# Sketched attention with a gated feed-forward on one core: weights loaded as fp32 and cast on chip, the first denominators made another way, and every engine's order written anew

## The chip, the cores and the metric

The kernel runs on one core of a Trainium2 chip. The metric is device microseconds of one launch; smaller is better. A core has TensorE (matrix products, in the profile PE, its weight loads PEld), VectorE (DVE), ScalarE (ACT), GpSimd (POOL) and SyncE (SP), which here only issues transfers. Products land in eight PSUM banks of 128 x 512 fp32. VectorE and ScalarE read them; GpSimd works here on SBUF alone.

## What is computed

Cut to what matters, the reference is:

```python
def phi(x):                       # S1, S2: 8 x 32
    a = einsum('rd,bhsd->bhsr', S1, x)
    b = einsum('rd,bhsd->bhsr', S2, x)
    return outer(a, b)            # 64 features for each row
q_p, k_p = phi(q), phi(k)         # q, k, v: 4 batches, 4 heads, 1088 rows, 32
kv  = einsum('bhsf,bhsd->bhfd', k_p, v)
z   = sum(k_p, axis=rows)
num = einsum('bhsf,bhfd->bhsd', q_p, kv)
den = einsum('bhsf,bhf->bhs', q_p, z) + 1e-6
x   = (num / den) as [4352, 128]
out = (relu(x @ w_gate) * (x @ w_val)) @ w_out      # 128 -> 1536 -> 128
```

## The kernel before

**Attention.** Rows of a batch lie in 34 columns of 32 rows on 128 partitions (four heads by 32). A batch's keys are transposed (`kt1`, lines 484 to 491), sketched with S1 and S2 (`ksk`, line 501), transposed back (`kt2`, line 507) and multiplied out to 64 features (`kphi`, line 543). `z` (line 515) sums the features, `w` and `wc` (528, 532) fold it back into a third sketch of 8 numbers, and `kv` (567) and `kve` (573) make the 64 x 32 table of each head. The queries follow (class Q): transposed (`qt1`, 987), sketched with three sketches at once (`qsk`, 780), transposed back (`qt2`, 793), and the denominator is a product and a sum of two of the sketches (`bw` 801, `red` 807, `rd` 811); `an` (815) divides, `qphi` (821) multiplies out, a transpose and `num` (848) give x, and ScalarE copies it to `xT` (861). The first half of batch 0 goes another way (class First, line 589), so that x is there sooner: its denominators come from `aT`, `csk` and a reciprocal that is spread over 32 columns and transposed (`rx`, `rT`), and `xd` (715) multiplies numerator and reciprocal.

**Feed-forward.** 4352 rows are cut into groups of 256 or 512 columns of `xT`. A unit (class F) is 512 columns of work: a gate product g and a value product v (line 916, each 512 columns in one or two matmuls), `relu` on ScalarE (921), the product of both, h, and four output matmuls o (944). h is one VectorE operation that reads v from PSUM (931), or, for the units in `POOL_UNITS`, a ScalarE copy of v (`vcp`, 925) and a GpSimd product (`hp`, 936). There are 102 units. Three blocks of each weight (g, v, o; t = 0 to 2) serve 512 hidden columns each. When a group has had its twelve hidden blocks, ScalarE scales the result (`oe`, 951) and four transfers store it.

**Weights.** Block 0 of each weight is loaded as fp32 by SyncE into tiles that are still free (`q_abc`) and cast by ScalarE (line 316). The other six are loaded by GpSimd's queue, which casts on the way (line 310). Their place is set by `RINGS`: behind the GpSimd product `kphi 0 8`, and a one-element GpSimd write called gate (line 391) keeps the load of batch 1's keys back until the fourth of them is issued.

**Order.** All operations are listed in one plan. `START` gives each a number; sorted by it they are emitted, and each engine takes its own in that order, strictly one after the other. `BANKS` gives each product its PSUM bank. `WARM` puts in matmuls of zeros (line 1015), 55 in all, 29 of them ahead of the first sketch.

Of the kernel before, what the change touches and what calls it, by code (L numbers as in the profile page):

```python
# [23 lines left out]
POOL_UNITS = [7, 8, 9, 10, 14, 15, 17, 23, 31, 43, 44, 47, 54, 64, 71, 74, 81, 94, 96]  # L24
KBC = [(2, 4), (4, 8)]
WL = {'g0': 'SP', 'v0': 'SP', 'o0': 'SP', 'g1': 'POOL', 'v1': 'POOL', 'o1': 'POOL', 'g2': 'POOL', 'v2': 'POOL', 'o2': 'POOL'}
V0L = [['SP', 'SP', 'SP', 'SP'], ['SP', 'SP', 'SP', 'SP']]
FILL = 'DVE'
RINGS = [['ld s1', 'ld s2', 'ld k01', 'ld v000', 'ld v001', 'ld v002', 'ld v003', 'ld v010', 'ld v011', 'ld v012', 'ld v013'], ['mz', 'kt1 0 0'], ['fills', 'kt1 0 0'], ['zero', 'fills'], ['ld k00', 'ld q00', 'table'], ['zero', 'mz'], ['zero', 'sel'], ['id32', 'masks', 's1r'], ['kphi 0 8', 'ld wv1', 'ld wg2', 'ld wg1', 'ld wv2', 'gate', 'ld wo1', 'ld wo2'], ['ld v013', 'ld wg0', 'ld wv0', 'ld q01']]
Q0E = 'ACT'  # L30
RXE = ['ACT', 'DVE']
START = [
# [68 lines left out]
]  # L101
WARM = {34: 29, 63: 2, 143: 14, 147: 1, 152: 9}


class Lease:
# [947 lines left out]
```

## Time and profile before

| what | value |
|---|---|
| time, three runs | 102.89, 101.67, 102.59 us; median 102.59 |
| profiled execution: span from the first to the last instruction | 100.1 us |
| first gate product on TensorE | 14.58 us |
| last output product done, ScalarE's last scaling starts | 96.62 us |
| busy: PE, DVE, ACT, POOL | 94.2, 82.7, 84.1, 65.8 us |
| bytes read and written in HBM | 9.05 and 2.23 MB |

The three times hold no span of their own, and the profiled execution no time of its own beside the span, so the 2.5 us between 100.1 and 102.59 is what lies around the span (start and end of a launch). The chain of waits is read backwards from the last instruction: what stands in it set the end. A row of the timeline has the start, the length, the engine, the line and the shapes. Lengths of neighbouring instructions of one engine overlap by some 0.06 us, so where many stand in a row the distance of their starts counts.

### The profile page before, as it was taken

The numbers are of one execution on the slowest core, as the hardware profiler recorded it, in microseconds if no ns is written. First come the engines' busy times: TensorE is split into PE (matmuls) and PEld (weight loads), VectorE is DVE, ScalarE is ACT, GpSimd is POOL, SyncE is SP. The second block draws the span as 40 slices with busy tenths as digits, with TensorE's granted clock in tenths as the row PEclk, the third lists the DMA queues.
The fourth block names the chain that finished last, engine by engine and source line by source line (L and its number), as shares of the span: only waits on it lengthen the run. The fifth ranks groups of instructions, "written<-read, shape, count | busy, mean of one in ns | idle before, by whom it ended". The sixth has DMA issues, their size and how long they took to land.

```text
span 100.1 us, 3180 instructions
## 1 busy us (share of the span) xinstructions
PE 94.2 (94%) x1223; PEld 68.3 (68%) x1223; DVE 82.7 (83%) x175; ACT 84.1 (84%) x169; POOL 65.8 (66%) x89
## 2 busy tenths in 40 slices
PE   6999989989999999999999999999999999999950
PEld 6978969848779965557673656765676665688940
DVE  4778779999989998999998689799746879897940
ACT  3445889999799798998999999899999999998730
POOL 6029947898988999999897699935944404001700
PEclk9999999999999999999999999999999999999999
DMA  2988889999930525208664200071217305003331
GB/s 43 370 229 267 146 122 358 339 269 276 342 125 0 111 66 134 45 12 235 165 182 99 60 0 7 1 169 27 52 29 120 78 0 129 2 7 84 99 105 52
DMA packets 14799, 12.40 MB, mean 124 GB/s; under 512 B 8256, under 2 KB 12352, under 8 KB 14784
## 3 DMA queue, kind: packets, MB, share of 16 engines
q1 hardware_dynamic: 13392, 10.70, 38.5%
q0 software_dynamic: 864, 0.79, 5.8%
q10 hardware_dynamic: 528, 0.72, 2.2%
q8 instruction: 9, 0.15, 0.7%
q14 instruction: 6, 0.05, 0.2%
HBM read 9.05 MB, written 2.23 MB: 113 GB/s over the span
## 4 chain that ended last, share of the span: by engine, by line
PE 81%; ACT 6%; POOL 4%; DMA 3%; issue 1%; DVE 1%
PE ps L916 42%; PE ps L944 23%; PE ps L1015 5%; ACT g_sb L921 4%; DMA wg<-in_moe_w_gate_dram 3%; PE ps L848 3%; PE ps L501 2%; PE ps L780 2%; POOL kp L543 2%; PE ps L567 2%; ACT v_sb L925 1%; POOL fqp L695 1%; ACT qpt L840 1%; PE ps L515 1%; POOL wv L310 1%
## 5 line engine op out<-in xcount | busy, mean ns | idle before, releaser
L921 ACT ACTIVATE g_sb<-ps 128x512 f16<-128x512 f32 x102 | 56.3, 613 | 3.9 <-PE ps L916 3.2
L931 DVE TENSOR_TENSOR ht<-g_sb,ps 128x512 f16<-128x512 f16 (+1 forms) x84 | 53.5, 673 | 7.2 <-PE ps L916 5.6
L916 PE MATMUL ps<-xT,wv 128*128 128x512 f16 (+1 forms) x132 | 35.6, 332 | 0.5 <-ACT g_sb L921 0.5
L916 PE MATMUL ps<-xT,wg 128*128 128x512 f16 (+1 forms) x132 | 34.3, 332 | 0.3 <-DMA wg<-in_moe_w_gate_dram 0.3
L944 PEld LDWEIGHTS <-ht 128*128 128x128 f16 x408 | 28.0, 98 | 9.2 <-issue 0.8
L944 PE MATMUL ps<-wo,ht 128*128 128x128 f16 x408 | 33.8, 219 | 0.0
L936 POOL TENSOR_TENSOR ht<-g_sb,v_sb 128x512 f16<-128x512 f16 x19 | 21.7, 1158 | 16.4 <-ACT g_sb L921 14.9
L916 PEld LDWEIGHTS <-wg 128*128 128x128 f16 x132 | 13.6, 115 | 5.9 <-issue 2.2
L543 POOL TENSOR_TENSOR kp<-kab 128x512 f16<-128x512 f32 (+2 forms) x14 | 15.7, 1136 | 2.0 <-DVE kab L507 2.0
L916 PEld LDWEIGHTS <-wv 128*128 128x128 f16 x132 | 13.9, 114 | 3.6 <-issue 1.3
L821 POOL TENSOR_TENSOR qqp<-qan,qabc 128x1024 f16<-128x1024 f32 (+1 forms) x9 | 14.9, 1658 | 0.4
L925 ACT CAST v_sb<-ps 128x512 f16<-128x512 f32 x19 | 11.3, 601 | 0.6 <-PE ps L916 0.5
L1015 PE MATMUL ps<-zero 128*128 128x128 f16 x55 | 5.9, 285 | 1.0 <-DVE zero L292 1.0
L793 DVE STREAM_TRANSPOSE qabc<-ps 128x128 f32<-128x128 f32 (+1 forms) x12 | 5.4, 488 | 1.0 <-PE ps L780 0.6
L987 DVE STREAM_TRANSPOSE qT<-q_sb 128x544 f32<-128x544 f32 (+2 forms) x9 | 5.9, 662 | 0.4 <-DMA q_sb<-in_q_dram 0.4
L1015 PEld LDWEIGHTS <-zero 128*128 128x128 f16 x55 | 5.1, 136 | 1.3 <-DVE zero L292 1.0
L951 ACT ACTIVATE o_sb<-ps 128x512 f32<-128x512 f32 (+1 forms) x10 | 5.2, 521 | 0.7 <-PE ps L944 0.7
L801 POOL TENSOR_TENSOR bw<-qabc 128x128 f32<-128x128 f32 (+1 forms) x9 | 3.7, 412 | 2.9 <-DVE qabc L793 2.9
L815 POOL TENSOR_TENSOR qan<-qabc,qrd 128x128 f32<-128x128 f32 (+1 forms) x9 | 3.3, 372 | 3.3 <-DVE qrd L811 3.3
L861 ACT CAST xT<-ps 128x512 f16<-128x512 f32 (+1 forms) x9 | 4.7, 517 | 0.5 <-PE ps L848 0.5
L491 DVE STREAM_TRANSPOSE kT<-k_sb 128x544 f32<-128x544 f32 x6 | 4.2, 724 | 0.0
L507 DVE STREAM_TRANSPOSE kab<-ps 128x576 f32<-128x576 f32 (+2 forms) x5 | 3.3, 664 | 0.7 <-PE ps L501 0.7
(94 smaller groups left out, 77.4 us busy)
## 6 DMA issues: line engine op xcount, KB each, us to landing
k_sb<-in_k_dram SPq DMA_DIRECT2D x3, 544.0 KB, 6.1
q_sb<-in_q_dram SPq DMA_DIRECT2D x3, 544.0 KB, 4.9
out_dram<-o_sb SPq DMA_DIRECT2D x22, 64.0 KB, 1.7
v<-in_v_dram SPq DMA_DIRECT2D x6, 144.0 KB, 7.7
v<-in_v_dram SPq DMA_DIRECT2D x6, 128.0 KB, 7.6
out_dram<-o_sb SPq DMA_DIRECT2D x16, 32.0 KB, 1.8
v<-in_v_dram SPq DMA_DIRECT2D x6, 64.0 KB, 3.1
k_sb<-in_k_dram SPq DMA_DIRECT2D x1, 288.0 KB, 3.5
```

The costliest lines, as they stand in the source:

```text
L543: eng.tensor_tensor(out=self.kp[:, lo:hi].rearrange("p x g (i a c) -> p (x g i) a c", i=2, a=R), in0=a[:, :, :, None].to_broadcast([128, n ...
L793: nc.vector.transpose(self.abc[:, lo:lo + m, 2 * i2:2 * i2 + 2].rearrange("p x h f -> p h x f"), pair(ls[i2])[:, :, lo * 32:(lo + m) * 32] ...
L821: nc.gpsimd.tensor_tensor(out=self.qp[:, lo:hi].rearrange("p x g (i a c) -> p (x g i) a c", i=2, a=R), in0=self.an[:, lo * H:hi * H, :, No ...
L916: nc.tensor.matmul(bank(l)[:, y * self.W:(y + 1) * self.W], w[:, j // 4, :, j % 4], x, start=True, stop=True, skip_group_check=True)
L921: nc.scalar.activation(out=self.gs, in_=bank(l), func=ACTF.Relu)
L925: nc.scalar.copy(out=self.vs, in_=bank(l))
L931: nc.vector.tensor_tensor(out=self.ht[:, t], in0=self.gs[:, t], in1=bank(l)[:, t], op=ALU.mult)
L936: nc.gpsimd.tensor_tensor(out=self.ht, in0=self.gs, in1=self.vs, op=ALU.mult)
L944: nc.tensor.matmul(o[:, s], self.ht[:, i * 128:(i + 1) * 128], wo[:, j // 4, j % 4], start=(j == 0 and s == 0), stop=(j == NJ - 1), skip_g ...
L951: nc.scalar.mul(out=self.os[:, 0:n * DM], in_=bank(self.lo)[:, 0:n * DM], mul=1.0 / (XSCALE * XSCALE))
L987: nc.vector.transpose(qT[b][:, lo:hi], q_sb[b][:, lo:hi])
L1015: nc.tensor.matmul(PS[:, 7, 0:128], zero, zero, start=True, stop=True, skip_group_check=True)
```

## The change

**Weights.** All nine blocks are loaded as fp32 by SyncE's queue. Five go into tiles of `q_abc`, four into `qT` of batches 2 and 3, which are used later. ScalarE casts g0, g1, g2, o1 and v2, GpSimd casts v0, v1, o0 and o2. The operations that later fill those tiles wait for the casts.

**First denominators.** The first half of batch 0 is taken in one piece of four columns (FN = 4) instead of two of two: one transposing of queries with a permuted view, one sketch, one transposing back, one `f aT` of 512 columns. The z product `f cT` keeps z in place and streams the queries, in four tiles of 32 partitions, so its result is transposed and needs one more VectorE transposing, `f tc`. The product `f bw` moves to GpSimd. Scratch for it lies in parts of `xT` and `v16` that are used later. The selector `s1r` is made by VectorE and ScalarE instead of ScalarE and GpSimd.

**Loads.** The ScalarE queue loads queries before keys. The gate is gone: batch 1's keys are the fifth transfer of SyncE's queue, ahead of most of batch 0's values, and batch 2's keys stand ahead of the first weight.

**Batch 0's features.** GpSimd makes `kphi 0 0` and `0 2`, VectorE `0 4` and a merged `0 6` (three columns, 768 wide).

**Orders.** `ORDER` and `BANKS` are new for every engine, `POOL_UNITS` has 22 units instead of 19, and there are 28 matmuls of zeros instead of 55 (20 ahead of the first sketch). VectorE takes one copy to `xT`, three scalings of results and the two value casts of batch 2 from ScalarE. All stores of groups go by SyncE.

On VectorE the place is the end of the way to the first x. Before, the rows up to the first `xd` (xT) are these; fbw, fdn and frd are the first denominators, kp_93 batch 0's features, bd its table:

```order
L680 TENSOR_TENSOR fbw<-fab,ps 128x8x8
L622 TENSOR_REDUCE fdn<-fbw 128x8
L624 RECIPROCAL frd<-fdn 128x8
L543 TENSOR_TENSOR kp_93<-kab_91,ps 128x512
L626 COPY frx<-frd 128x256
L987 STREAM_TRANSPOSE qT_87<-q_sb_76 128x576
L573 TENSOR_TENSOR bd<-ps,maskg 128x128
L715 TENSOR_TENSOR xT<-ps,frT 128x256
```

Nothing in them belongs to another batch. In the changed kernel the rows up to the first `xd` are these (kab_92 is batch 1, kT_85 here batch 2, zs_347 batch 1, qabc_112 the second half of batch 0):

```order
L593 STREAM_TRANSPOSE kab_92<-ps 128x2x9x2x16
L686 STREAM_TRANSPOSE fc<-ps 128x128
L1050 STREAM_TRANSPOSE qT_87<-q_sb_76 128x576
L693 TENSOR_REDUCE fdn<-fbw 128x16
L609 TENSOR_TENSOR zs_347<-ps,mz 128x32
L695 RECIPROCAL frd<-fdn 128x16
L628 TENSOR_TENSOR kp_93<-kab_91,ps 128x512
L858 STREAM_TRANSPOSE qabc_112<-ps 128x2x2x32
L577 STREAM_TRANSPOSE kT_85<-k_sb_74 128x544
L649 TENSOR_TENSOR bd<-ps,maskg 128x128
L858 STREAM_TRANSPOSE qabc_112<-ps 128x2x2x32 x3
L722 TENSOR_TENSOR xT<-ps,xT 128x256
```

One transposing of batch 2's keys, the transposing back of batch 1's and four of the second half of batch 0 now stand ahead of the first `xd`; a little earlier both transposings of batch 1's keys (kT_86) do too.

On GpSimd the place is from batch 0's features to the weights. Before (wv, wg, wo are casting loads, fqp and qqp query features of batch 0):

```order
L543 TENSOR_TENSOR kp_93<-kab_91 128x512
L543 TENSOR_TENSOR kp_93<-kab_91 128x256
L310 DMA wv<-in_moe_w_val_dram 128x512
L695 TENSOR_TENSOR fqp<-fab 128x512
L310 DMA wg<-in_moe_w_gate_dram 128x512 x2
L695 TENSOR_TENSOR fqp<-fab 128x512
L310 DMA wv<-in_moe_w_val_dram 128x512
L391 MEMSET k_sb_75 1x1
L801 TENSOR_TENSOR bw<-qabc_111 128x8x8
L310 DMA wo<-in_moe_w_out_dram 128x512 x2
```

In the changed kernel, behind the two fqp and two kp_93 (kp_94 is batch 1's features, the CASTs are weights):

```order
L689 TENSOR_TENSOR fbw<-fab,fc 128x16x8
L628 TENSOR_TENSOR kp_94<-kab_92 128x768
L628 TENSOR_TENSOR kp_94<-kab_92 128x512
L866 TENSOR_TENSOR bw<-qabc_112 128x8x8
L628 TENSOR_TENSOR kp_94<-kab_92 128x512 x2
L880 TENSOR_TENSOR qan_118<-qabc_112,qrd_134 128x64
L866 TENSOR_TENSOR bw<-qabc_112 128x8x8
L329 CAST wv<-qabc_113 128x512
L886 TENSOR_TENSOR qqp_122<-qan_118,qabc_112 128x512
L329 CAST wv<-qabc_115 128x512
L329 CAST wo<-qabc_114 128x512
```

All of batch 1's features, which before came behind the first two GpSimd products of units, now stand ahead of the first value weight.

The core of the diff (tables of numbers cut):

```diff
-POOL_UNITS = [7, 8, 9, 10, 14, 15, 17, 23, 31, 43, 44, 47, 54, 64, 71, 74, 81, 94, 96]
-KBC = [(2, 4), (4, 8)]
-WL = {'g0': 'SP', 'v0': 'SP', 'o0': 'SP', 'g1': 'POOL', 'v1': 'POOL', 'o1': 'POOL', 'g2': 'POOL', 'v2': 'POOL', 'o2': 'POOL'}
+POOL_UNITS = [4, 8, 9, 14, 17, 23, 24, 25, 44, 52, 57, 63, 65, 67, 69, 72, 74, 89, 91, 92, 93, 96]
+FN = 4
+KD = [4, 6]
+ORDER = [
+    16, 4, 0, 38, 37, 36, 1, 2, 3, 6, 14, 40, 15, 48, 39, 8, 9, 146, 7, 41, 10, 42, 66, 11, 147,
...
-WARM = {34: 29, 63: 2, 143: 14, 147: 1, 152: 9}
+WARM = {41: (20, 128), 147: (2, 128), 91: (6, 128)}
...
-        eng = WL[f"{kind}{t}"]
-        if eng == "POOL":
-            op = P.add("POOL", f"ld w{kind}{t}", lambda: nc.gpsimd.dma_start(out=dst, in_=src))
-            return op, op
+        raw = stage[n]
+        ld = load(f"ld w{kind}{t}", "SP", lambda eng: eng.dma_start(out=raw, in_=src))
+        e = on(f"cw {kind}{t}", "ACT")
+        op = P.add(e, f"cw {kind}{t}", lambda: CP[e](out=dst, in_=raw),
+                   [ld] + ([ftab] if e == "ACT" else []))
+        (staged[3 - n // 2] if n < 5 else stagedT[3 - (n - 5) // 2]).append(op)
...
-    g_op = P.add("POOL", "gate", lambda: nc.gpsimd.memset(k_sb[1][0:1, 0:1], 0.0))
...
-                at = P.add("PE", f"f aT {y}", lambda y=y, l=lat: self.at(l, y), [qt1[y], s1r_op],
-                           take=[lat])
+            at = P.add("PE", f"f aT {n}", lambda: nc.tensor.matmul(
+                bank(lat)[:, 0:n * 128], s1r.rearrange("p r h i -> p (r h i)"), qT[0][:, 0:n * 128],
+                start=True, stop=True, skip_group_check=True), qt1 + [s1r_op], take=[lat])
...
+            ct = P.add("PE", f"f cT {n}", lambda: self.ct(lc), [kk.zc_op, ate], take=[lc])
+            tc_ = P.add("DVE", f"f tc {n}", lambda: nc.vector.transpose(
+                self.c.rearrange("p x f -> p (x f)"), bank(lc)[:, 0:n * 32]), [ct], drop=[lc])
+            be = on(f"f bw {n}", "DVE")
+            bw = P.add(be, f"f bw {n}", lambda: VE[be].tensor_tensor(
...
+        def ct(self, lc):
+            for a in range(4):
                 nc.tensor.matmul(
+                    bank(lc)[32 * a:32 * a + 32, 0:self.n * 32],
+                    self.kk.zs.rearrange("p h r -> p (h r)"), self.by_a(f_aT, a),
+                    start=True, stop=True, skip_group_check=True)
```

More of the change, by code (lines that the diff above doesn't have):

```diff
@@ L185 @@
     P = Plan()
+    QE = {"SP": nc.sync, "ACT": nc.scalar, "POOL": nc.gpsimd}
+    CP = {"ACT": nc.scalar.copy, "DVE": nc.vector.tensor_copy, "POOL": nc.gpsimd.tensor_copy}
+    VE = {"DVE": nc.vector, "POOL": nc.gpsimd}
     def bank(l, i=0):
@@ new lines, in later @@
+        def later(self, pk, pu):
+            b = self.b
+            t1s = [P.add("DVE", f"kt1 {b} {c}", lambda c=c: self.t1c(c), [lk[b]] + pk)
+                   for c in range(2)]
+            la = Lease(P, 2)
+            s = P.add("PE", f"ksk {b} 0", lambda: self.sk(la, 0, KX, KCOL), t1s + [ws_op, f2],
+                      take=[la])
+            self.sks.append(s)
+            self.abs.append(P.add("DVE", f"kt2 {b} 0", lambda: self.t2(la, 0, KX), [s] + pu,
+                                  drop=[la]))
+            return [(lo, hi, self.abs[:1], None) for lo, hi in [(0, 2), (2, 4), (4, 6), (6, KX)]
+                    ], t1s, False
@@ L995, with t1f @@
-    qs = [Q(0, GX, [(0, 2), (2, 2)], 0, [ks[0]], [t0r], [], True)]
-    qx[0, 4], qx[0, 6] = qs[0].x_ops
-    tr1 = [t0r]
-    lq[3].after += qt1 + [t0r]
+    def t1f():
+        nc.vector.transpose(
+            qT[0][:, 0:FN * 128].rearrange("p (y e a c) -> p y a e c", y=FN // 2, e=2, a=4),
+            q_sb[0][:, 0:FN * 128].rearrange("p (y a e c) -> p y a e c", y=FN // 2, a=4, e=2))
+    qx, cutq, tr1 = {}, [], []
+    if FN:
+        qt1 = [P.add("DVE", f"qt1 0 f{FN}", t1f, lq0[:1])]
+        fg = First(ks[0], qt1)
+        for y in range(FN // 2):
+            qx[0, 2 * y] = fg.x_ops[y]
+        for b in (2, 3):
+            for o in vcs[b]:
+                o.after += fg.uses
+        if FN == 2:
+            cutq = [(QY, 2 * QY, lq0[:1])]
+    else:
+        cutq = [(0, 2 * QY, lq0[:1])]
```

499 lines of the change are left out of this document (263 added, 236 removed), and 141 rows, old and new, of tables (BANKS, ENG, ORDER, START).

## The prediction, as it was put on record

> **What bounds the kernel now.** I read the page first, then the busy time by stretches, the chain of waits in order of time, and the first 30 us of the timeline.
>
> ```profile
> span 100.1 us, 3180 instructions
> PE 94.2 (94%) x1223; PEld 68.3 (68%) x1223; DVE 82.7 (83%) x175; ACT 84.1 (84%) x169; POOL 65.8 (66%) x89
> GB/s 43 370 229 267 146 122 358 339 269 276 342 125 0 111 66 134 45 12 235 165 182 99 60 0 7 1 169 27 52 29 120 78 0 129 2 7 84 99 105 52
> ```
>
> The last row has 40 slices of 2.5 us; the loads come back to it.
>
> ```profile
> 70.00:80.00 10.00, 10.00 (x96) 6.49 (x96) 6.90 (x11) 9.66 (x21) 5.78 (x5) 1.00 0.37 70
> 80.00:90.00 10.00, 10.00 (x98) 6.73 (x96) 8.76 (x14) 9.72 (x20) 1.16 (x1) 1.00 0.14 34
> ```
>
> In each ten microseconds the columns are PE, PEld, DVE, ACT, POOL. PE is never idle, but ACT is at 97%, so which of them sets the pace must be read from the chain:
>
> ```profile
> 11.26 3.28 DMA wg<-in_moe_w_gate_dram
> 14.58 0.63 PE ps L916 x4
> ...
> 16.01 1.57 ACT g_sb L921 x3
> ...
> 28.15 0.65 PE ps L501 x16
> ...
> 31.34 0.89 PE ps L944 x16
> 32.23 0.31 PE ps L515 x16
> ...
> 37.91 0.73 PE ps L780 x32
> ...
> 82.56 1.29 PE ps L916 x6
> ```
>
> From 21 us on nearly every piece is TensorE, back to back: a product of 512 columns takes 1.29/6 = 0.215 us, an output product 0.89/16 = 0.0556. So **TensorE sets the end from some 25 us on**, and a microsecond is won only by starting its work earlier, by leaving it less work, or by fewer waits. The head has three parts that are not its own: the wait for wg, ScalarE's relus, and what makes the first x:
>
> ```profile
> 13.93 0.42 DVE L715 TENSOR_TENSOR xT<-ps,frT 128x256 f16<-128x256 f32 x1 [0.47 <-PE ps L708]
> 15.62 0.60 PE L916 MATMUL ps<-xT,wv 128*128 128x256 f16 x4
> 21.93 0.40 PE L944 MATMUL ps<-wo,ht 128*128 128x128 f16 x4
> 96.62 0.38 ACT L955 ACTIVATE o_last<-ps 128x256 f32<-128x256 f32 x1 [1.02 <-PE ps L944]
> ```
>
> The first x is there at 14.35, the first gate product starts at 14.58 (a cast load), the first value product at 15.62, the first output product at 21.93, and TensorE is done at about 96.6.
>
> **Ledger of TensorE before.** 102 units (the relu row below has their count) of 2 x 0.215 + 4 x 0.0556 = 0.652 make 66.6 us. Attention behind 14.58: three `ksk` of 0.65, three z of 0.31, three `qsk` of 0.7, and from the smaller pieces of the same chain 5.8 for `kv`, `num`, `w`, transposes and the tail rows: 11.1. Together 77.7 of the 82.0 us from 14.58 to 96.6, so 4.3 us are waits. The products up to 33.5 us split them:
>
> ```profile
> 0.00:33.50 33.50, 12.34 (x88) 8.85 (x88) 1.00 0.78 216
> 0.00:33.50 33.50, 4.73 (x59) 3.98 (x60) 1.00 0.78 216
> ```
>
> These are lines 916 and 944 alone: 88 products of 256 columns (9.5 us) and 59 outputs (3.3). What is left, 53.8, and 6.8 of attention are 60.6 of the 63.1 us to 96.6. So about 2.5 us of waits lie behind 33.5, some tenths at each change between kinds of products, and 1.8 ahead of it.
>
> **The change part by part.** Durations, lengths of one in ns behind the comma:
>
> ```profile
> L921 ACT ACTIVATE g_sb<-ps 128x512 f16<-128x512 f32 x102 | 56.3, 613 | 3.9 <-PE ps L916 3.2
> L931 DVE TENSOR_TENSOR ht<-g_sb,ps 128x512 f16<-128x512 f16 x82 | 52.8, 679 | 7.2 <-PE ps L916 5.6 <-POOL qan L815 0.6 <-ACT g_sb L921 0.2
> L936 POOL TENSOR_TENSOR ht<-g_sb,v_sb 128x512 f16<-128x512 f16 x19 | 21.7, 1158 | 16.4 <-ACT g_sb L921 14.9 <-ACT v_sb L925 1.5
> L543 POOL TENSOR_TENSOR kp<-kab 128x512 f16<-128x512 f32 x10 | 10.6, 1073 | 1.5 <-DVE kab L507 1.5
> L543 POOL TENSOR_TENSOR kp<-kab 128x768 f16<-128x768 f32 x3 | 4.5, 1512 | 0.4 <-DVE kab L507 0.4
> L987 DVE STREAM_TRANSPOSE qT<-q_sb 128x544 f32<-128x544 f32 x6 | 4.2, 720 | 0.0
> L491 DVE STREAM_TRANSPOSE kT<-k_sb 128x544 f32<-128x544 f32 x6 | 4.2, 724 | 0.0
> L507 DVE STREAM_TRANSPOSE kab<-ps 128x576 f32<-128x576 f32 x3 | 2.3, 783 | 0.5 <-PE ps L501 0.5
> L793 DVE STREAM_TRANSPOSE qabc<-ps 128x128 f32<-128x128 f32 x6 | 1.5, 286 | 0.4 <-PE ps L787 0.3
> L695 POOL TENSOR_TENSOR fqp<-fab 128x512 f16<-128x512 f32 x2 | 2.3, 1146 | 0.0
> L316 ACT CAST wv<-qabc 128x512 f16<-128x512 f32 x1 | 0.6, 622 | 0.0
> masks.py:197 POOL MEMSET id<- 128x128 f32 x1 | 0.2, 206 | 0.3 <-POOLq L1037 0.3
> ```
>
> *The first x comes later.* VectorE's first transposing can start as now, and it waits for `ws` as now:
>
> ```profile
> 3.58 0.71 DVE L484 STREAM_TRANSPOSE kT<-k_sb 128x512 f32<-128x512 f32 x1
> 5.33 0.19 DVE L370 TENSOR_TENSOR wS<-ps,maskp 128x32 f32<-128x32 f32 x1 [0.70 <-ACT wq L375]
> ```
>
> Before, 2 us of waits lie between 3.58 and the first `xd`; the new order fills them and more. From `ws` at 5.4, in the new order and by distances of starts (0.06 less than lengths): two `kt1` 1.4, `f t2`, sb and two `kt2` 1.5 (to 8.3), batch 1's `kt1` 1.35, zc and the merged `kphi` 1.1 (10.7), batch 1's `kt2` 0.7, `f tc` 0.25, batch 0's last `qt1` 0.75 (12.4), red, zc, rd 0.6, `kphi` 0.65 (13.65), four `qt2` 0.93, one `kt1` of batch 2 0.68, `kve` 0.23 (15.55), `xd` 0.38: **15.9 instead of 14.35**. Some 3.7 of this is other batches' work. ScalarE is as late: `f rd` is there at 13.0, then two `rx`, a copy of pt, casts of g2, g1, g0 at 0.55 to 0.6 each and two rT copies fill it until 16.8, when the first relu can start (15.03 now). First gate product **16.0**: +1.4.
>
> *What was moved ahead of it* no longer has to be done behind it: `ksk` 1 0.65, z 1 0.31, w 1 0.3, second `f num` 0.22: -1.5. This leaves 76.2.
>
> *The value weights.* A GpSimd cast of 128x512 is in no row. Below stands ScalarE's 0.62, above GpSimd's two-input product of 1.16; the write of 128x128 takes 0.206, four times that 0.82. I take 0.9, nearest to that write. GpSimd gets `f t2` at 7.2; then fqp, kp, fqp, kp (4.3), fbw 0.45 (12.15), two of batch 1 2.55, bw at 15.1, two of batch 1 2.1 (17.55), an and bw 0.65, v1 to 19.1, qqp 1.05, **v0 to 21.05, o0 to 21.95**. So the first value product is at 20.5 instead of 15.62 (transposings of batch 2 and a sketch of batch 1 stand ahead of it on TensorE), the first h at 21.6 instead of 16.11, the first output product at 23.6 instead of 21.93. Behind the casts on GpSimd wait the second half of batch 0 and the first `hp`, for which `o 4` waits, all within these 2 us.
>
> The Trainium skill (GPSIMD Engine Reference, Engine selection) says that a one-input operation there runs at roughly line rate, a two-input one at half: it would put the cast near 0.6. By that the walk's v0 comes 0.6 us earlier and the sum falls by about as much. No run here shows it yet.
>
> *Waits of TensorE after.* Walking both orders: from 16.0 to 25 it has 6.6 us of work that it may start (18 products, two outputs, `ksk` 2, `qsk` 1, z 2), so it waits 2.4. From 25 to 33.5 relus, h and freed banks come about as fast as it works: 0.3. By then 38 products (8.2), 12 outputs (2.7) and 3.9 of attention are done, 61.4 is left; the later waits scale with the attention that is left, 5.5 of 6.8: 2.1. Sum 4.8 instead of 4.3: +0.5.
>
> *What costs nothing.* ScalarE's two more casts, three more `vcp`, and less scaling, copying and casting (which go to VectorE) cancel within 0.5 us; from 33.5 on it has 57.5 us of work in 63, VectorE 53.5. Without that slack each microsecond more on ScalarE would be one at the end. The stores have the old tail. The loads: ahead of and with g0, the last gate block, lie 3.58 MB; at the mean of the second to fourth slice, 289 GB/s, it lands at 1.6 + 12.4 = 14.0, needed at 15.9; v0 1.6 MB later at 350 (358 and 339 in the row), 18.6, needed at 20.2. The casting loads on GpSimd's queue go (six issues of some 0.57 us), but the new casts take as long.
>
> **Sum**: +1.4 - 1.5 + 0.5 = +0.4 us on a span of 100.1, and on the median 102.59: **103.0 us**, no change that can be told.
>
> **Rivals.** *Faster, 100.4 us.* The work moved ahead pays twice: with batches 1 and 2 prepared, TensorE finds no change of kind to wait at, the 2.1 us behind 33.5 fall to 0.5, and the casts take 0.62, which takes 1.0 off the wait to 25: 0.4 - 1.6 - 1.0 = -2.2. For it: VectorE is some 1.4 us further by 33.5 than now. Against it: the waits behind 33.5 stand at TensorE's own changes of operands, which stay.
>
> *Slower, 105.0 us: the value weights come too late.* At 1.16 a cast, and by full lengths rather than distances (16 operations at 0.05), v0 is cast at 22.4 and o0 at 23.5; the first outputs slip 1.35, the outputs of blocks 0 and 2 0.55 more, and nothing behind gives it back, since TensorE is then full: 0.4 + 1.9 = +2.3. It decides once v0's cast ends after 22.6. For it: strict order on GpSimd. Against it: 0.206 for the write.
>
> *The loads are not earlier, 105.0 us.* At the mean of the first five slices, 211 GB/s, g0 lands at 18.6 and not at 14.0; that the casting loads slowed those slices (146 and 122) speaks against it. The first relu stands behind g0's cast on ScalarE and slips by 2.7; TensorE regains 0.7 from its waits: with the 0.4, +2.4.
>
> *TensorE stays slow for long, 105.4 us.*
>
> ```profile
> 1.00 3.28 PE L1015 MATMUL ps<-zero 128*128 128x128 f16 x29 [1.00 <-DVE zero L292]
> 10.41 0.67 PE L1015 MATMUL ps<-zero 128*128 128x128 f16 x9
> ```
>
> The first 29 products of zeros take 113 ns each, later ones half; now 20 stand ahead of the sketches instead of 29, and 14 behind the first sketch are gone. If the fast rate came only with the dense work at 20 us, the 5 us of work until then would take double, of which 2.4 fall into waits: +0.4 + 2.4. The Trainium skill (TensorE: Matmul & The Clock Gate, The HAM clock gate) has this as a rule: half rate until some 3.4 us of sustained work. Against it: the sketches and products of z fill TensorE from 7.8 to 10.9.
>
> **How the numbers follow.** About as forecast 0.50; faster 0.24; late value weights 0.14; late loads 0.07; slow clock 0.05. The forecast's own range, with casts from 0.62 to 1.16 and 1 us on either side for the walk, is 101.4 to 104.4. The rivals lie at 100.4 and up to 105.4; with their own spread, 100.2 to 105.8 leaves out 2 in 10. Two per cent, about what a measurement can tell from no change, is 100.5 and 104.6: faster 0.24, same 0.50, slower 0.26.
>
> **What would show it.** Right: the first gate product at 16.0 +- 0.6, `xd` ending at 15.9; v0's cast ending near 21 and a GpSimd cast near 0.9; the first output product near 23.6; the chain all TensorE behind 26; products of 256 columns at 0.108 from 16 us on. Wrong: a first gate product before 15, which would say that VectorE's queue has slack that I don't see; TensorE waiting behind 35 us; ScalarE idle for a weight's transfer; 113 ns for 128 columns behind 10 us.

## The result, and the profile after

The changed kernel took 109.17, 110.46 and 112.72 us, median 110.46, against 102.59: a ratio of 1.073 (95% interval 1.057 to 1.089), **slower**. The forecast was 103.0 with a range to 105.8. Executions of one kernel scatter, so a ratio here compares only those within 1.5% of the shortest of their kernel, while a median is that of all. The profiled execution took 109.17 us, with a span of 107.3 (100.1 before). So 1.9 us lie around the span here (1.8 in the other two executions), and not the 2.5 that "Time and profile before" works out from two different executions. Lines have moved: 916 is now 980 (gate and value products), 944 is 1008 (outputs), 793 is 858 and 507 is 593 (transposing reads of the two sketches, qt2 and kt2), 1015 is 1095 (zeros).

From the page of the changed kernel, the span and the busy time:

```profile
span 107.3 us, 3089 instructions
PE 93.8 (87%) x1174; PEld 65.7 (61%) x1174; DVE 83.7 (78%) x171; ACT 82.7 (77%) x170; POOL 68.8 (64%) x89
```

TensorE is busy as long as before (93.8 against 94.2 us, though with 27 products of zeros fewer), and the other engines nearly so. Its last product ends at 102.70, so it stands idle for 102.70 - 93.8 = 8.9 us on the way there; before it was 96.6 - 94.2 = 2.4. **The 7.2 us of the span are 6.5 us of idle time of TensorE and 1.1 of a longer tail** (4.6 instead of 3.5 us behind the last output), less 0.4 of busy time. The busy time by stretches (PE, PEld, DVE, ACT, POOL) shows that the end is as dense as before, and where it isn't:

```profile
18.00:22.00 4.00, 3.04 (x78) 1.66 (x76) 3.02 (x7) 3.90 (x9) 3.63 (x6) 1.00 1.09 267
22.00:25.00 3.00, 1.40 (x14) 1.24 (x14) 1.92 (x5) 0.62 (x2) 0.86 (x2) 1.00 1.08 286
37.00:40.00 3.00, 2.06 (x30) 0.90 (x28) 2.39 (x6) 1.52 (x4) 2.21 (x3) 1.00 0.36 86
50.00:55.00 5.00, 4.00 (x33) 2.49 (x32) 4.85 (x7) 3.73 (x8) 5.00 (x5) 1.00 0.46 112
...
80.00:90.00 10.00, 10.00 (x92) 6.89 (x91) 8.44 (x14) 10.00 (x21) 3.48 (x3) 1.00 0.22 56
```

From 22 to 25 us no engine is busy for even two thirds of the time: everybody waits for somebody. The chain that ended last was TensorE back to back from 21 us on before; now there are transfers, VectorE's transposing reads and even a store in it:

```profile
2.39 5.88 DMA k_sb<-in_k_dram
11.02 7.08 DMA qabc<-in_moe_w_val_dram
18.12 4.14 DMA v<-in_v_dram
22.26 0.72 DVE qabc L858
23.02 0.83 PE ps L980 x6
23.87 0.73 DVE qabc L858
...
44.84 0.58 SPq L277
46.41 2.00 DMA out_dram<-o_sb
```

What TensorE waited for, in total, with the number of waits and the longest (its longest rows):

```profile
PE ps L1095 <- DVE zero L307: 2.6, 1, 2.6
PE ps L980 <- DVE qabc L858: 1.5, 2, 1.0
PE ps L845 <- DVE kab L593: 1.0, 1, 1.0
PE ps L980 <- DVE kab L593: 0.9, 1, 0.9
PE ps L980 <- DVE ht L995: 0.8, 1, 0.8
PE ps L614 <- DVE qabc L858: 0.6, 1, 0.6
```

The whole list of the kernel before:

```profile
PE ps L1015 <- DVE zero L292: 1.0, 1, 1.0
PE ps L916 <- ACT g_sb L921: 0.5, 2, 0.4
PE ps L916 <- DMA wg<-in_moe_w_gate_dram: 0.3, 1, 0.3
PE ps L528 <- DVE bd L573: 0.2, 1, 0.2
```

Two things stand out. The zeros start at 2.6 us instead of 1.0. And gate and value products, a fold (614) and a sketch (845) wait for transposing reads of other sketches (858, 593) whose result they do not use; with outputs (0.4) and a reconstruction of x (0.2) these waits are 4.6 us. The list of the kernel before has no such row. The signposts of the prediction, from the timeline of TensorE:

```profile
17.76 1.03 PE L980 MATMUL ps<-xT,wg 128*128 128x256 f16 x8
...
23.02 0.60 PE L980 MATMUL ps<-xT,wg 128*128 128x256 f16 x4 [1.03 <-DVE qabc L858]
23.45 0.38 PE L980 MATMUL ps<-xT,wv 128*128 128x256 f16 x2
...
24.64 0.41 PE L614 MATMUL ps<-zs,L 128*128 128x32 f32 x2 [0.58 <-DVE qabc L858]
```

The first `xd` ends at 17.71 (forecast 15.9), the first gate product is at 17.76 (16.0), the first value product at 23.45 (20.5); the first output product is at 27.32 (23.6).

### The profile page after: what moved, and what is told of

Read it like the earlier page. It is cut to its first block, busy times and chain, and to the rows that moved or that the text cites. A ratio compares the mean times of both kernels' runs of the same rounds, so it can differ in the third digit from the quotient of the medians.

```text
span 107.3 us, 3089 instructions
## 1 busy us (share of the span) xinstructions
PE 93.8 (87%) x1174; PEld 65.7 (61%) x1174; DVE 83.7 (78%) x171; ACT 82.7 (77%) x170; POOL 68.8 (64%) x89
## 4 chain that ended last, share of the span: by engine, by line
PE 60%; DMA 18%; DVE 5%; SPq 5%; POOL 3%; ACT 2%; issue 2%; ACTq 0%; DVEq 0%
PE ps L980 36%; PE ps L1008 19%; DMA qabc<-in_moe_w_val_dram 7%; DMA k_sb<-in_k_dram 5%; DMA v<-in_v_dram 4%; DVE qabc L858 3%; DMA out_dram<-o_sb 2%; POOL qqp L886 2%; PE ps L643 1%; PE ps L913 1%; DVE ht L995 1%; SPq L327 1%; ACT g_sb L985 1%; POOL ht L1000 1%; SPq L277 1%
## 5 line engine op out<-in xcount | busy, mean ns | idle before, releaser
L995 DVE TENSOR_TENSOR ht<-g_sb,ps 128x512 f16<-128x512 f16 (+1 forms) x81 | 51.6, 673 | 9.0 <-ACT g_sb L985 5.0
L1000 POOL TENSOR_TENSOR ht<-g_sb,v_sb 128x512 f16<-128x512 f16 x22 | 25.3, 1156 | 16.3 <-ACT v_sb L989 13.2
L980 PE MATMUL ps<-xT,wv 128*128 128x256 f16 (+1 forms) x132 | 33.5, 331 | 0.5 <-DVE qabc L858 0.5
L628 POOL TENSOR_TENSOR kp<-kab 128x512 f16<-128x512 f32 (+1 forms) x14 | 16.1, 1164 | 0.0
L858 DVE STREAM_TRANSPOSE qabc<-ps 128x128 f32<-128x128 f32 (+1 forms) x12 | 6.0, 509 | 3.7 <-PE ps L980 1.7
L1095 PE MATMUL ps<-zero 128*128 128x128 f16 x28 | 3.5, 311 | 2.6 <-DVE zero L307 2.6
L761 POOL TENSOR_TENSOR fqp<-fab 128x512 f16<-128x512 f32 x2 | 2.1, 1069 | 5.1 <-DVE Sb L404 5.1
L1017 ACT ACTIVATE o_sb<-ps 128x256 f32<-128x256 f32 (+1 forms) x7 | 3.4, 490 | 2.5 <-DMA out_dram<-o_sb 2.0
L1050 DVE STREAM_TRANSPOSE qT<-q_sb 128x544 f32<-128x544 f32 (+1 forms) x7 | 4.9, 716 | 0.0
L1095 PEld LDWEIGHTS <-zero 128*128 128x128 f16 x28 | 2.7, 143 | 2.7 <-DVE zero L307 2.6
L643 PE MATMUL ps<-v,kp 128*128 128x64 f16 x72 | 4.2, 193 | 0.0
```

Of the source, the lines that this page charges most:

```text
L628: eng.tensor_tensor(out=out.rearrange("p x g (i a c) -> p (x g i) a c", i=2, a=R), in0=a[:, :, :, None].to_broadcast([128, n, R, R]), in1= ...
L643: nc.tensor.matmul(m[:, 64 * p:64 * p + 64], self.kp[:, x, p], v16[self.b][:, 2 * p:2 * p + 2, x * D:(x + 1) * D], start=(x == 0 and p == ...
L858: nc.vector.transpose(self.abc[:, lo:lo + m, 2 * i2:2 * i2 + 2].rearrange("p x h f -> p h x f"), pair(ls[i2])[:, :, lo * 32:(lo + m) * 32] ...
L980: nc.tensor.matmul(bank(l)[:, y * self.W:(y + 1) * self.W], w[:, j // 4, :, j % 4], x, start=True, stop=True, skip_group_check=True)
L995: nc.vector.tensor_tensor(out=self.ht[:, t], in0=self.gs[:, t], in1=bank(l)[:, t], op=ALU.mult)
L1000: nc.gpsimd.tensor_tensor(out=self.ht, in0=self.gs, in1=self.vs, op=ALU.mult)
```

## The experiments

### The head: zeros too late, and too few

The change also moved VectorE's write of the tile of zeros behind its other fills, and the stretch of zeros became 20 products instead of 29. The TensorE rows up to 11 us of the changed kernel:

```profile
2.60 2.32 PE L1095 MATMUL ps<-zero 128*128 128x128 f16 x20 [2.60 <-DVE zero L307]
...
8.37 2.08 PE L678 MATMUL ps<-qT,s1r 128*128 128x512 f32 x2
10.38 0.53 PE L601 MATMUL ps<-kab 128*32 128x32 f32 x18
...
13.37 0.38 PE L601 MATMUL ps<-kab 128*32 128x32 f32 x18
```

The same 18 products of z take 0.53 us at 10.38 and 0.38 at 13.37: the engine is slow up to about 11.5 us, although the granted clock reads 1.00 throughout and it hardly idles (from 2.60 to 14.30 us it is busy for 11.34 of 11.70). `e1_early_zeros` writes the zeros first and issues 34 of them:

```diff
-WARM = {41: (20, 128), 147: (2, 128), 91: (6, 128)}
+WARM = {41: (34, 128), 147: (4, 128), 91: (6, 128)}
```

and the number of `zero` stands first in VectorE's order. Expected:

> The changed kernel with VectorE's memset of the zeros first on its queue (it is the sixth) and 34 + 4 products of zeros ahead of the first sketches instead of 20 + 2. Theory 'slow TensorE' (until some 11.5 us TensorE runs at about half its rate: the two products of L678 take 1.04 us each, z of batch 0 0.53 where that of batch 1 takes 0.38): the pair of L678 takes 1.2 us or less, z of batch 0 ends before 9.8 instead of 10.9, the first xd ends at 16.7 instead of 17.7, first gate product near 16.8; but VectorE's L858 for batch 1 still waits until 22.2 for a load, so the time falls by 0.3 to 1.0 us only. Rival 'the pair is long by its shape': the pair stays at 2.1 us, first gate product after 17.4, time within 0.3 us of the changed kernel's 110.5.

Measured: 107.16 us, ratio 1.041 [1.032, 1.050]. Its rows:

```profile
0.99 3.36 PE L1095 MATMUL ps<-zero 128*128 128x128 f16 x34 [0.99 <-DVE zero L307]
...
7.08 1.12 PE L678 MATMUL ps<-qT,s1r 128*128 128x512 f32 x2
8.14 0.38 PE L601 MATMUL ps<-kab 128*32 128x32 f32 x18
...
16.40 1.20 PE L980 MATMUL ps<-xT,wg 128*128 128x256 f16 x8
```

The two products of 512 columns take 1.12 us instead of 2.08, z 0.38 instead of 0.53, and the first gate product comes at 16.40 instead of 17.76. The gain, 3.3 us of the median, is more than was expected. The two profiled executions, 109.17 and 107.65 us, differ by 1.5, of which 1.36 are there at the first gate product; where the other 1.8 of the medians come from, in executions without a trace, is not shown.

The control is `e11_before_late_zeros`: the kernel *before* with its zeros written behind the fills and with 20 and 2 of them, as in the change.

```diff
-WARM = {34: 29, 63: 2, 143: 14, 147: 1, 152: 9}
+WARM = {34: 20, 63: 2, 143: 2, 147: 1, 152: 9}
```

> The kernel before with VectorE's memset of the zeros behind the other fills and 20 + 2 products of zeros instead of 29 + 14, as in the change; nothing else. Theory 'slow TensorE': its eight products of L666 take about 2 us instead of 1.16, the first gate product slips by 0.8 to 1.5 us, and the time rises by 0.8 to 2 us to 103 to 104. Rival 'the zeros only fill a wait': first gate product within 0.4 us of 14.6 and the time within 0.5 us of before.

Its four executions took 104.84, 107.97, 108.03 and 108.33 us beside 101.99 of the kernel before; they lie too far apart for a ratio, but each is at least 2.8 us longer. In the profile, of the execution of 108.03:

```profile
3.56 2.32 PE L1015 MATMUL ps<-zero 128*128 128x128 f16 x20 [3.56 <-DVE zero L292]
...
20.75 0.60 PE L916 MATMUL ps<-xT,wg 128*128 128x256 f16 x4 [0.16 <-DVE xT L715]
```

The first gate product slipped from 14.58 to 20.75 in it; the execution of 104.84 us has no trace. So late and fewer zeros are enough to slow the kernel before, too, by 2.8 us at least; how much as a rule stays open. Both edits change the time of the zeros and their number together, and TensorE's first products with S stand behind the zeros in its order, so what is delay and what is a slow engine is not told apart.

### First ideas for the waits of TensorE: a shared counter, the stores

At 22.25 us the read L858 itself waited for a transfer of values which it does not use:

```profile
22.25 0.72 DVE L858 STREAM_TRANSPOSE qabc<-ps 128x512 f32<-128x512 f32 x1 [1.24 <-DMA v<-in_v_dram]
```

My first theory was that a tile for staged weights (`qabc` of batch 1) is to blame. `e2_own_stage` stages that block elsewhere:

```diff
-             for i, e in ((3, 0), (3, 1), (2, 0), (2, 1), (1, 0))]
+             for i, e in ((3, 0), (3, 1), (2, 0), (2, 1))] + [xT[:, 1024:2048].bitcast(FP32)]
```

> The changed kernel with the fp32 copy of value block 1 staged in the unused batch 1 half of xT instead of qabc 1, which L858 of batch 1 writes. Theory 'shared counters' (L858 waits on one of eight counters that SP's loads share in turn, and is let go only by the later v load on the same counter): L858's idle time of 1.24 us on DMA v goes, the first L858 of batch 1 starts near 21.0 instead of 22.26, TensorE's idle time of 1.6 us between 22 and 25 falls below 0.8, and the time falls by 0.7 to 1.3 us. Rival 'L858 had to wait for the sketch of batch 1 or for GpSimd's cast anyway': it starts after 21.8 and the time stays within 0.3 us.

Measured: 110.41 us, 1.066 [1.058, 1.074]. The read no longer waits for the transfer, yet stands at 23.00, since it now waits 1.13 us for the z product of TensorE (601), which writes a bank between the two that it reads (next section); no difference to the change can be told. In the change that z product ended at 22.00, so the transfer held the read up by 0.25 us at most. **The theory falls** as the cause of the loss.

`e3_store_bufs` answers the store in the chain with a fourth buffer for results:

```diff
-    f_o = ctx.enter_context(tc.tile_pool(name="f_o", bufs=3))
+    f_o = ctx.enter_context(tc.tile_pool(name="f_o", bufs=4))
```

> The changed kernel with four output buffers instead of three. Theory 'stores stuck behind others in SP's order hold the buffers': ScalarE's copy of the fourth group no longer waits 2.0 us at 46.5 for a store, the DMA step at 46.4 leaves the chain, TensorE's idle time between 50 and 55 falls from 1.0 below 0.4, and the time falls by 1.0 to 2.0 us. Rival 'TensorE waits there for GpSimd's qqp and the transposes behind it': the same stretch stays idle for 0.8 us or more and the time moves by less than 0.5 us.

Measured: 111.52 us, 1.095 [1.086, 1.104]. The store at 46.4 us has left the chain, and ScalarE's longest wait for a store (1.97 us at 102.25, ahead of its last scaling but one) is 0.5, but the time is not lower: **this is not the cause of the loss** either. What the buffer is worth can't be told from this run, since all its executions have a mean granted clock of 0.963 to 0.978 (last section), which may be why they are longer. `e4_three`, the three edits together, took 108.09 us, 1.0465 [1.038, 1.055]: no more than the zeros alone.

> All three edits together: early zeros, own stage for value block 1, four output buffers. If each is a loss of its own they add: first gate product near 16.8, L858 of batch 1 before 20.5, no wait of ScalarE for a store at 46, and 107.0 us (106.0 to 108.0). If one wait only hides the next, as 'the order of everything else sets the pace' has it, the sum is less than half of that: 109 us or more.

### The table of banks

The next idea was the table that the diff hides as numbers. A sketch is a pair of PSUM banks, and VectorE reads both in one transposing instruction. Before, all 17 pairs are neighbours, such as (3,4). After, nine of 16 are apart: (0,3) twice, (0,5), (2,7), (1,6), (0,4), (4,6), (0,2), (1,7). The program sets its waits for the memory that an instruction touches; for a read of banks 1 and 6 that is the whole stretch, banks 1 to 6. The waits of the compiled program show it (DVE_49 and Activation_49 are its names for the counters of VectorE and ScalarE). The gate product of 23.02 us writes bank 4, last read by a relu of ScalarE, and waits for VectorE, whose count is that of the read of banks 1 and 6:

```
174 L980 MATMUL ps_72<-xT_95,wg_82 128x256 [waits DVE_49]
```

`e5_adjacent` gives every pair two neighbouring banks, in a table of its own:

```diff
-    (0,), (1,), (1,), (3,4), (5,6), (6,), (6,), (5,), (0,), (7,), (2,3), (2,), (2,), (5,), (0,3),
...
+    (3,), (4,), (0,), (0,1), (6,7), (6,), (6,), (5,), (0,), (0,), (1,2), (1,), (1,), (5,), (3,4),
...
```

> The changed kernel, same order on every engine, with another table of banks in which all sixteen two-bank sketches lie in neighbouring banks (nine of them do not in the changed kernel: 0 and 3, 0 and 5, 2 and 7, 1 and 6 and so on). Theory 'a transposing read of two banks far apart blocks the banks between them, since waits are set for the whole stretch': TensorE's idle time that ends with L858 or L593 (4.6 us in the profile of the changed kernel, in six places) falls to 1.5 or less, first output product 1 to 2 us earlier, and the time falls by 3.0 to 4.5 us to about 106.5. Rival 'those waits are for the banks' own earlier users or for TensorE's operands': idle time stays above 3 us and the time within 1.2 us of 110.5.

Measured: 108.35 us, 1.053 [1.044, 1.061]. In its list of waits only 0.2 us on the read L593 are left of the 4.6. With the early zeros as well (`e6_zeros_adjacent`) 107.54, 1.0525 [1.044, 1.061]: no more than either alone. A new table changes every reuse of a bank, so this was not clean.

> Early zeros and neighbouring banks together. If slow TensorE in the head and blocked banks are the two main losses: 102.5 to 104.0 us (107.2 with early zeros alone), first gate product at 16.4, first output product near 24, no stretch of 2.5 us behind 30 us with more than 0.3 us of idle TensorE but one at 50 to 55, where VectorE's cast of v takes 1.9 us beside GpSimd. Rival 'late loads keep the pace': TensorE still waits for value blocks and q of batch 1, 105.5 us or more.

`e7_before_spread` is the control: the kernel before, with its banks only renamed (0 to 7 become 1, 4, 0, 3, 6, 2, 5, 7), so that order, work and every reuse are the same, but all pairs lie two to four banks apart.

```diff
-    (0,), (2,), (3, 4), (5, 6), (1,), (5,), (3,), (7,), (6, 7), (5,), (2,), (6,), (5, 6), (6,),
...
+    (1,), (0,), (3,6), (2,5), (4,), (2,), (3,), (7,), (5,7), (2,), (0,), (5,), (2,5), (5,), (5,),
...
```

> The kernel before with its banks renamed (0 to 7 become 1, 4, 0, 3, 6, 2, 5, 7), nothing else: same order, same distances between uses of a bank, but every two-bank sketch now lies in banks 2 to 4 apart. Theory 'blocked banks': slower than before by 2 to 4 us (104 to 106.5), with TensorE idle behind transposes of L793 and L507. Rival 'the numbers of banks are only names': within 0.5 us of before.

Measured: 109.13 us, 1.071 [1.064, 1.078]. A renaming alone costs 7%. Its profiled execution was longer than those compared (114.67 us against 108.58 to 109.34), with a late transfer of queries and a granted clock of 0.50 from 12 to 18 us, so only the causes in its list are read, none of which the kernel before has:

```profile
PE ps L916 <- DVE qabc L793: 1.4, 3, 0.6
PE ps L944 <- DVE qabc L793: 1.3, 2, 0.7
...
PE ps L501 <- DVE qabc L793: 0.8, 1, 0.8
```

With three smaller rows on these reads they are 4.5 us. The compared executions are some 7 us longer than the kernel before and have no trace, so how the rest of the 7% comes about is not seen.

If the stretch is the reason, two reads of one bank each need no renaming back. `e14_spread_split` is e7 with each two-bank read written so (the same in the other two reads):

```diff
-            nc.vector.transpose(
-                self.abc[:, lo:lo + m, 2 * i2:2 * i2 + 2].rearrange("p x h f -> p h x f"),
-                pair(ls[i2])[:, :, lo * 32:(lo + m) * 32].rearrange("p h (x f) -> p h x f", f=32))
+            for y in range(2): nc.vector.transpose(
+                self.abc[:, lo:lo + m, 2 * i2 + y],
+                bank(ls[i2], y)[:, lo * 32:(lo + m) * 32].rearrange("p (x f) -> p x f", f=32))
```

> The kernel before with its banks renamed (109.1 us) and every transposing read of two banks split into two reads of one. Theory 'a read of two banks far apart blocks those between': back to 102 to 103.5, the time of the kernel before and some tenths for 16 more instructions. Rival 'some banks are slower or clash': 107.5 or more.

Measured: 102.80 us in ten runs, 1.0039 [1.0004, 1.0075], with none of these waits in its list. The same renaming costs 7% with two-bank reads and 0.4% without: **that the two-bank reads are the cause is shown**.

`e12_split_reads` does the same to the changed kernel, table and order untouched:

> The changed kernel with each transposing read of two banks (L593, L858) written as two reads of one bank each; order and table of banks untouched. Theory 'blocked banks': TensorE no longer waits for L858 or L593 at products whose own bank is free, its idle time behind these two lines falls from 4.6 us to 1.5 or less, and the time falls to 105.5 to 107.5, less some 0.1 us of VectorE for each of 16 more instructions. Rival 'the gain with neighbouring banks came from the other changes in that table': 109.5 or more.

Measured: 107.19 us, 1.053 [1.041, 1.065], span 104.2. The gate product now waits for the relu, and for nothing else:

```
178 L980 MATMUL ps_72<-xT_95,wg_82 128x256 [waits Activation_49]
```

and in the timeline it starts at 21.76 instead of 23.02, without a wait:

```profile
21.76 0.63 PE L980 MATMUL ps<-xT,wg 128*128 128x256 f16 x4
```

All rows on L858 and L593 are gone from TensorE's list. In time, the interval still touches that of the change, so the size is better read with the zeros: `e13_split_zeros`, e12 and e1 together, took 105.20 us, 1.026 [1.014, 1.0375].

> Split reads and early zeros in the changed kernel, its own order and banks otherwise. If the two losses are apart and the table of neighbouring banks of the earlier run was just a poorer table: 103.0 to 105.5 (107.2 with early zeros alone). Rival 'behind both stands a third limit, the loads': 106 or more, with TensorE idle between 18 and 25 us for q of batch 1 and value block 0.

### What is left of the loss

About 2.6% remain. The two longest waits of TensorE in e13's list, for an h and for a cast gate weight:

```profile
PE ps L980 <- DVE ht L995: 1.2, 1, 1.2
PE ps L980 <- ACT wg L329: 1.0, 1, 1.0
```

*The value casts of batch 2* went to VectorE. There one of them takes 1.70 us, started while a GpSimd product runs until 53.01; the other, started 0.01 us ahead of a GpSimd product, takes 0.45:

```profile
51.06 1.95 POOL L886 TENSOR_TENSOR qqp<-qan,qabc 128x1024 f16<-128x1024 f32 x1
51.63 1.70 DVE L634 CAST v<-v 128x576 f16<-128x576 f32 x1
55.64 0.45 DVE L634 CAST v<-v 128x576 f16<-128x576 f32 x1
```

`e8_adj_vc` (e6 with both on ScalarE) took 107.54 us, 1.047 [1.038, 1.056]: no difference told from e6. `e16_v_and_stores` (e13, both casts on ScalarE, four output buffers) took 104.82, 1.017 [1.007, 1.027]: the best, not told apart from e13.

> Early zeros, neighbouring banks, and the two casts of batch 2's v back on ScalarE (the change has them on VectorE, where one of them took 1.70 us and the other 0.45, the long one beside a GpSimd product of 1.95). Theory 'VectorE's cast waits for GpSimd': the idle second of TensorE at 53 us goes, and the time is 0.5 to 1.0 us below that without this edit. Rival 'ScalarE is as full as VectorE there': no difference, within 0.3 us.

> Split reads and early zeros (105.2 us), ScalarE for both casts of batch 2's v and four output buffers. TensorE's 0.94 us of idle time from 50 to 55, ahead of which VectorE's cast takes 1.9 us beside GpSimd, falls below 0.3; the wait for a store at 43 goes; time lower by 0.5 to 1.3 us. Rival 'as with neighbouring banks, ScalarE is the later one there': within 0.3 us.

*Work of other batches ahead.* `e9_own_batch_first` moves batch 1's queries and batch 2's keys and queries behind the first outputs and the loads of weights ahead; `e10_casts_first` also moves GpSimd's value casts up. Both have early zeros, ScalarE's casts of the values, and a new table of neighbouring banks.

> On top of early zeros, neighbouring banks and ScalarE's casts of v (107.5 us): the weights' loads ahead of k of batch 2 and q of batch 1, q of batch 2 behind all other loads of batch 1 and 2, and the work on them (transposes, sketches and z of batch 2's keys, both sketches of queries) behind the first output products instead of ahead of them. Theory 'other batches' loads and work stand ahead of batch 0's own first outputs': value block 0 is cast before 19 instead of after 22, first output product before 23, TensorE idle from 12 to 33.5 us falls from 3.4 us below 1.5, and the time falls to 102.5 to 104. Rival 'the loads are all done by 30 us either way, so their order gives nothing': 106.5 us or more.

> As the run before, with GpSimd's casts of value blocks 1 and 0 and output block 0 ahead of its products of batch 1's keys (2 x 1.06 us) and of the second half of batch 0. Theory 'GpSimd's queue holds the value weights': first value product and first output product 1 to 2 us earlier than in the run before, time lower by 0.5 to 1.5 us. Rival 'the casts wait for their loads': the casts start when their loads land, GpSimd idles before them, no gain (within 0.3 us) or a loss up to 1 us, since batch 1's keys come later.

Measured: 117.00 us, 1.135 [1.124, 1.146], and 117.99, 1.152 [1.143, 1.160]. The first output product of e9 is at 23.55, just where the forecast had it, and the time is the worst but one of all:

```profile
25.00:30.00 5.00, 3.13 (x60) 2.22 (x60) 3.08 (x6) 2.06 (x4) 0.51 (x1) 1.00 0.99 299
30.00:60.00 30.00, 24.41 (x335) 16.49 (x334) 23.06 (x46) 21.17 (x43) 21.67 (x22) 1.00 0.27 69
```

What was put off comes back as waits between 18 and 60 us. In its list 3.1 us of the waits of the feed-forward's products end on the reads 858 and 593, though every pair is adjacent, so neighbouring banks alone don't rule such waits out. With so much reordered by hand, this does not say which step of the original order costs; it does say that an early first output is not what sets the end.

*The loads.* In e13 GpSimd's casts wait for their transfers:

```profile
19.27 0.61 POOL L329 CAST wv<-qabc 128x512 f16<-128x512 f32 x1 [0.99 <-DMA qabc<-in_moe_w_val_dram]
22.11 0.61 POOL L329 CAST wv<-qabc 128x512 f16<-128x512 f32 x1 [1.21 <-DMA qabc<-in_moe_w_val_dram]
23.46 0.61 POOL L329 CAST wo<-qabc 128x512 f16<-128x512 f32 x1 [0.74 <-DMA qabc<-in_moe_w_out_dram]
```

`e15_weights_first` puts the loads of g0, v1, v0 and o0 ahead of batch 2's keys and batch 1's queries, and the transposing of those keys behind the second `xd`; `e17_all` adds e16's edits.

> Split reads and early zeros (105.2 us), and the loads of the last gate block, value blocks 1 and 0 and output block 0 ahead of k of batch 2 and q of batch 1 (2 x 0.56 MB); VectorE's two transposes of that k go behind the second xd so that its queue doesn't wait for them. Theory 'late loads': the last gate block lands near 15.5 instead of 17.2, TensorE's 1.0 us wait at 17 goes, value block 0 is cast by 19.5 instead of 22.7, first output product by 23 instead of 24.8, and the time falls by 0.7 to 1.5 us. Rival 'TensorE has other batches' work to fill in meanwhile, and gives it back later': idle time to 33.5 falls but the time stays within 0.3 us.

> All of these together: 102.5 to 103.7 us if the gains add, at the kernel before or just above it; 104 or more if the order of the rest, made for waits that did not come as planned, keeps the pace.

Measured: 108.22 us, 1.055 [1.047, 1.064], and 1.049 [1.039, 1.059] for e17, whose median is 107.86 us without a fourth execution of 501 us (108.50 with it). e15's casts start at 18.18, 19.76 and 20.31 and wait for nothing. But the keys land later, and TensorE, whose order has their sketch ahead of the value products, waits for them:

```profile
20.36 0.79 PE L587 MATMUL ps<-kT,wS 64*32 64x288 f32 x16 [3.07 <-DVE kT L577]
```

So this order of the loads does not help. From 18 to 25 us the transfer engines are busy all the time (the shares of 1.09 and 1.08 in the windows above), and what goes first made something else late here. The price of the loads stays open: in e15's profile the granted clock is 0.50 from 22 to 24 us, behind that wait, and its executions have a mean of 0.961 to 0.984, which is a loss of its own; no other order of the loads was tried with e13's edits.

## Why the prediction was wrong, point by point

**"Sum 4.8 instead of 4.3: +0.5", the waits of TensorE.** This is the step that failed most: measured +4.4. In the terms of the sum, the 7.2 us of the span are 3.2 at the first gate product (forecast 1.4), 1.1 in the tail (forecast 0), the -1.5 of work moved ahead, and the waits: from 17.76 to 102.70 are 84.9 us, less the 76.2 of work 8.7, against 4.3 before. (Idle time in the trace says the same: 5.6 us behind the first gate product against 1.1, so of the 4.3 that I called waits 1.1 were idle.) I walked the orders of five engines, but treated the banks as free whenever their last reader was done. The diff said that all banks are new, and I never read the table. Nine pairs of banks lie apart, so a read stands in the way of products that use the banks between; 4.6 us of TensorE's time end on such reads, and the control shows that this alone can cost 7%. With the reads split and nothing else changed (e12), the same stretch is 81.8 us, from 18.13 to 99.94, which leaves 5.6 of waits, near the 4.8 of the forecast. In measured ratios it is worth 1.5 to 2.0 points of the 7.3, by e12 against the change and e13 against e1; the intervals there are wide. No rival named it: it would have been "slower, because more reads hold more banks", to be seen in the table alone.

Four sums of the working are off, none by enough to matter: the pieces of attention add up to 10.8 and not 11.1, those named from 16.0 to 25 us to 6.0 and not 6.6, GpSimd's walk to `fbw` to 11.95 and not 12.15, and in the rival of the slow TensorE 5 us less 2.4 are 2.6.

**"First gate product 16.0".** Measured 17.76. The order was walked rightly, but with durations of a fast TensorE, such as 1.0 us for the two products of `f aT`, which took 2.08. With early zeros it came at 16.40, within the 0.6 that I allowed; 1.36 of the 1.8 us came with the zeros. **The rival "TensorE stays slow for long"** had 0.05. Its mechanism was right and its stretch too, in part: slow to 11.5 us, not to 20 (to 19.4 in the profile of e11). It was dismissed because sketches and z "fill TensorE from 7.8 to 10.9"; in the changed kernel they filled it at half rate. I had seen that 20 zeros replace 29 and not that VectorE writes them 1.6 us later. It brings 3.2 points by e1 against the change and 2.7 by e13 against e12. The rival deserved more than 0.05. The rule of the Trainium skill (TensorE: Matmul & The Clock Gate, The HAM clock gate), half rate until some 3.4 us of sustained work, speaks for this rival, and e1 agrees with it: 3.36 us of unbroken zeros leave a fast engine at 4.3 us. The change does not: TensorE goes on almost without a gap behind its 2.32 us of zeros, so by the rule it would be fast from some 6.0 us, an estimate (2.60 and 3.4), but it is slow to about 11.5. Which products count as sustained work no run here shows.

**"0.9 a cast" on GpSimd.** Measured 0.61 in all four. The estimate near 0.6 from the sentence of the Trainium skill (GPSIMD Engine Reference, Engine selection) on one-input operations was right, and my nearest row was not: a memset of 128x128 scaled by four. It hardly mattered, since GpSimd came to the casts late: `fbw` had waited 1.96 us for VectorE's `fc` and started at 13.63 instead of 11.7. So v1 ended at 20.04, v0 at 21.63, o0 at 23.01, against 19.1, 21.05 and 21.95.

**"The loads cost nothing".** g0 was to land at 14.0 and v0 at 18.6. In e13 the last of the three g casts waits for its transfer until 17.26 and v0's cast until 22.11, so both are some 3 us later than that; in the change itself TensorE and GpSimd were late enough that only o0's cast waited, 0.76 us. The rival "the loads are not earlier" had 0.07 and the right direction. What it costs can't be told: e15 removed the waits of GpSimd's casts and got others.

**"The stores have the old tail".** 4.6 us instead of 3.5; one execution each, and ScalarE's last scaling but one waited 1.97 us for a store. The profiles of the other runs with three buffers have tails of 3.3 to 4.3 us, those with four (e3, e4, e16) of 3.2 to 3.8, so part of the 1.1 may be the buffers; in time it was not told apart.

**"Cancel within 0.5 us"** for ScalarE and VectorE holds in busy time (82.7 and 83.7 us against 84.1 and 82.7); the value cast of 1.70 us was not foreseen and no difference in time could be told (e8).

**What bounds the kernel** was right: TensorE is nearly full from 60 to 90 us in both (29.5 and 30.0 us of 30), and what it idles earlier is not made up. Of the 7.3%, by the ratios, the zeros bring about 3 and the reads of two banks about 2. Between the profiled executions it is the other way, 1.2 to 1.5 us for the zeros and 2.9 to 3.2 for the reads, so which is larger is not settled. The last 2.6% (1.4 to 3.75) **stay open**: late transfers and the single waits for h, features and weights in e13 are seen, but no experiment separated them, and no version was faster than the kernel before.

## What to carry to other kernels

Read every table of resources in a diff, not only the orders: in the waits of a program like this one, an access that spans several banks counts for all banks between its first and its last, so keep such pairs adjacent or read them one at a time. Look at the first microseconds of TensorE on the timeline, in durations of one known instruction, since the granted clock did not show the slow start here, and treat what makes the warm-up work possible (here the write of a tile of zeros) as part of the critical path. An operation prepared early is not free where transfers are saturated: it moves the wait.

## What the runs showed of the hardware that was not expected

*A slow TensorE with granted clock 1.00.* In the first 11 us of the change, products took up to twice their later time (2.08 against 1.12 us for the same pair), while the profile gives 1.00. The reading itself is no guide: two profiled executions of kernels with the order of the kernel before, of e11 and of e7, did nearly the same from 12 to 18 us, four transposes taking 1.17 us in both (0.71 before), with granted clocks of 1.00 and 0.50:

```profile
12.00:18.00 6.00, 6.00 (x56) 5.64 (x57) 3.71 (x12) 2.43 (x8) 3.33 (x6) 1.00 0.73 102
12.00:18.00 6.00, 6.00 (x60) 5.64 (x60) 3.51 (x11) 2.43 (x7) 3.14 (x6) 0.50 0.75 122
```

*A granted clock of 0.50 in the middle.* All executions of e3 had a mean clock of 0.963 to 0.978; the profile of one shows where:

```profile
24.00:30.00 6.00, 5.62 (x29) 3.65 (x28) 3.63 (x8) 3.21 (x7) 1.92 (x3) 0.50 1.05 255
```

In 6 us TensorE did 29 instructions there, against 63 in the same stretch of the change. It appears in some executions only (two of the three of the change had a mean clock of 0.977) and not always there: from 22 to 24 us in the profile of e15, behind a wait of 3.07 us, and from 12 to 18 in that of e7. What sets it off was not tried. So a part of the difference between two kernels can be this, where their executions do not all have a clock near 1.

*A VectorE cast of fp32 to fp16 started while a GpSimd product ran* took 1.70 us instead of 0.45 (2.27 in e12 and e13, started together with it), and ended 0.32 us behind that product.
